# Scaling x and w_in so that the halves of g need no factor, and a list scheduler that knows more of its transfers

## The chip, the cores and the metric

The kernel runs on one core of a Trainium2 chip (trn2). The metric is the device time of one execution in microseconds. TensorE (PE) multiplies matrices, VectorE (DVE), ScalarE (ACT) and GpSimd (POOL) do elementwise work, SyncE (SP) issues nearly all transfers. Each engine runs its own queue of instructions in order and waits for others by semaphores.

## What is computed

```python
def _attn_ref(q, k, v):                      # (8, 8, 576, 64) each
    k_p = k.reshape(B, H, Sp, pool, D).mean(axis=3)      # pool = 8, Sp = 72
    v_p = v.reshape(B, H, Sp, pool, D).mean(axis=3)
    attn = softmax(np.matmul(q, k_p.transpose(0, 1, 3, 2)) / np.sqrt(D))
    return np.matmul(attn, v_p)
def _moe_ref(x, w_in, w_out, alpha):         # 4608 tokens, 512 -> 2048 -> 512
    h = x @ w_in
    g = np.maximum(h, 0.0) + alpha * np.minimum(h, 0.0)
    return g @ w_out
def _moe2_ref(x, w_gate, w1, w2):            # 8 experts, 512 -> 1024 -> 512, top 1
    logits = x @ w_gate
    ...
        h = np.maximum(xe @ w1[e], 0.0)
        out[mask] = gate_w[mask, None] * (h @ w2[e])
```

The three stages follow each other: the attention's output is x of the first, dense feed-forward block ("first MoE"), and that one's output goes to one of eight experts for each token ("second MoE").

## The kernel before

**Numbers.** Every matrix product is made of three float16 products: an operand a is split into a high half hi = f16(a s) and a low half lo = f16(a s - hi), and hi hi + hi lo + lo hi is summed in PSUM. `s_hi` (L183 on ACT, L185 on DVE, L187 on POOL) and `s_lo` (L198 on DVE; L200 and L201, two instructions, on POOL) make the halves. The scale s comes from a maximum over the operand: `inv_of` gives inv = max * 2^-14 and s = 1/inv; `over_all` takes a maximum over all partitions through a small matmul (tile `mp`, L308) and DVE (`dg` L304, `mr` L311).

**Stages.** Up to about 150 us w_in and w_out, which come as float64, are loaded, turned into float32 (L709 to L725; `w_in_t`, `w_out_t`), their maxima taken (L178, `absmax`) and split into `w_in_hl` and `w_out_hl`. w_in has four groups of columns with a scale each (`sw`), w_out one scale. The first MoE goes by 18 blocks of 256 tokens. `plan_tile` makes the attention of 128 tokens: q is loaded (`qr`, L528), scaled and split (`qs`), transposed by a transfer (`qT`), multiplied (`sc`), exponentiated on ACT (L574), normalised and split into `Abuf`, transposed (`AT`, L605) and multiplied with v (`xp`); its output is split into `xT`. `plan_in` makes 16 blocks `hp` of h (L804); for each two of them ACT makes relu(-h) (`r`, L818), DVE makes the activation in place (L822), then comes the high half of g (`gT`, by `s_hi` with the group's factor `cg`) and the low half (by `s_lo`). `r` has two buffers, `hp` three. `plan_out` multiplies with w_out (`yp`, L846) in four quarters. `plan_gate` splits the output (`x`), transposes it (`x2T`, L879), computes the gate (`gp`, L910), ranks the tokens (`rp`) and writes a table. `plan_expert` meanwhile splits the experts' weights (`ew` to `eo`) and stores them (`wsc`). From 1004 us on `plan_slots` takes 128 tokens at a time: it reads the table (`srec`, L1244), gathers (`x2g`, L1251), transposes (`x2gT`, L1264), multiplies with `ws` (L1276 and L1294) and scatters.

**Order.** Nothing of this is written in its final order. Each `plan_*` function adds operations to a plan, with the engines that may do them, an estimated duration, what they wait for, a key and the pools they take from and give back. `Plan.emit` is a list scheduler: it keeps a clock for each engine, takes the operation that can start first (ties by key), picks the engine, and so writes each engine's queue. SP's transfers have a rule of their own there, given by

```python
            if o.eng == "SP":
                dma = max(dma, t + 1.1) + o.dur
                e["t"] = max(t + 0.5, dma - AHEAD)
                o.end = dma + 0.95
```

so every transfer holds SP for 0.5 us and lands 0.95 us after its share of the DMA engines' time. The estimates set only the order; on the chip each instruction starts when its data are there.

Of the kernel before, what the change touches and what calls it, by code (L numbers as in the profile page):

```python
# [13 lines left out]
ACTF = mybir.ActivationFunctionType  # L14
# [18 lines left out]
class Op:  # L33
    __slots__ = ("eng", "dur", "fn", "deps", "key", "lat", "acq", "rel", "n", "users", "est", "end")
# [5 lines left out]
class Plan:  # L40
# [6 lines left out]
    def add(self, eng, dur, fn, deps=(), key=0.0, lat=0.0, acq=(), rel=(), order=()):  # L47
        o = Op()
        o.eng, o.dur, o.fn, o.key, o.lat, o.acq, o.rel = eng, dur, fn, key, lat, acq, rel
# [10 lines left out]
    def emit(self):  # L60
# [13 lines left out]
        while left:  # L74
# [57 lines left out]
def attn_moe_moe_kernel(ctx: ExitStack, tc: tile.TileContext, q, k, v, w_in, w_out, alpha,  # L132
# [263 lines left out]
    def alpha_c():  # L396
        mr = sm_["mr"]
        V.tensor_copy(cw[:, 0:1], mr[:, 0:1])
# [15 lines left out]
    def plan_batch(b, dl, users):  # L414
# [5 lines left out]
        for w in range(2):  # L420
            for c in range(nc_):
# [18 lines left out]
                o = add("SP", dmat(72 * 2048 * hn), load, key=dl - 28 + (8 * w + c) * 8 / nc_, acq=[(pl, 1)])  # L440
# [54 lines left out]
        oKT[b] = add("SP", 1.2, kT, [o2, o3, o4], key=dl - 4 - SPQ, acq=[("KT", 1)], rel=[("kc", 1)])  # L495
# [3 lines left out]
        o3 = add("SP", 0.5, vdma, [o1], key=dl - 4)  # L499
# [19 lines left out]
    def plan_tile(i):  # L519
# [99 lines left out]
        def xhi():  # L619
            if half == 0:  # L620
                xTt[j] = wk.tile([128, 2, KD, TB], F16, tag="xT", name="xT", bufs=2)
            s_hi(xTt[j][:, 0, :, sl], c["xp"], S14)

        def xlo():
            s_lo(xTt[j][:, 1, :, sl], xTt[j][:, 0, :, sl], c["xp"], S14)

        ends = [b for b in bs if LAST[b] == i]
        o = add("SP", dmat(262144) * 1.85, load, key=first(dl - 30, -6), acq=[("q", 1), ("att", 1)])
# [6 lines left out]
        o = add("SP", 1.0, q4, [o], key=dl - 16 - SPQ, acq=[("qT", 1)], rel=[("qs2", 1)])  # L635
# [13 lines left out]
        o = add("SP", 1.8, aT, [o1, o2], key=dl - 7 - SPA, acq=[("AT", 1)], rel=[("A", 1)])  # L649
# [8 lines left out]
    def plan_w(src, name, col, dl0, dl1, after):  # L658
# [83 lines left out]
        for g in range(ng):  # L742
# [8 lines left out]
            def scale(mg=mg, ig=ig, sg=sg):  # L751
                inv_of(mg, ig, sg)
# [15 lines left out]
        oW[name + "_s"] = add("DVE", tiny(4), scales3, o_s + [o_alpha, oW.get("w_in_s")], key=dl0 + 1)

        p1 = None  # L770
        for c in range(8):
            d = {}
            g = c * ng // 8

            def hi(eng, c=c, d=d, g=g):
# [18 lines left out]
    def plan_in(j):  # L794
        for m in range(KF):
# [651 lines left out]
```

## Time and profile before

| | |
|---|---|
| time, median of 3 runs | 1445.33 us (1442.6 to 1445.35) |
| the profiled execution | 1447.14 us, span 1445.4 us |
| PE busy | 1266.9 us (88%) |
| DVE, ACT, POOL busy | 891.2, 592.7, 778.7 us (62, 41, 54%) |
| mean granted TensorE clock | 0.972 of full speed |

Shares of busy time are means over stages with different limits. An idle time is put down to the instruction whose semaphore came last, the releaser. A line of a helper, as L178 or L198, stands for many operations; the tile tells which one is meant. Half the clock's full speed is the lower of TensorE's two levels.

### The profile page before, as it was taken

The numbers are of one execution on the slowest core, as the hardware profiler recorded it, in microseconds if no ns is written. First come the engines' busy times: TensorE is split into PE (matmuls) and PEld (weight loads), VectorE is DVE, ScalarE is ACT, GpSimd is POOL, SyncE is SP. The second block draws the span as 40 slices with busy tenths as digits, with TensorE's granted clock in tenths as the row PEclk, the third lists the DMA queues.
The fourth block names the chain that finished last, engine by engine and source line by source line (L and its number), as shares of the span: only waits on it lengthen the run. The fifth ranks groups of instructions, "written<-read, shape, count | busy, mean of one in ns | idle before, by whom it ended". The sixth has DMA issues, their size and how long they took to land. (4 is left out here: it accounts for less than half of the span.)

```text
span 1445.4 us, 30543 instructions
## 1 busy us (share of the span) xinstructions
PE 1266.9 (88%) x11555; PEld 875.0 (61%) x11555; DVE 891.2 (62%) x2051; ACT 592.7 (41%) x1324; POOL 778.7 (54%) x847
## 2 busy tenths in 40 slices
PE   0157799889898989999899999999799999999997
PEld 0145455646655755666576667765676776777674
DVE  7998788779667968868877777654252332332222
ACT  3786555536454645645564556541010110110010
POOL 6788967668677867647665666464122122112111
PEclk9998999999999999999999999999999999999999
DMA  9983397766777766676577476536658843593334
GB/s 241 290 196 91 98 222 149 191 152 163 190 149 171 201 190 130 176 195 153 126 189 199 122 149 146 172 103 197 168 133 240 198 91 74 167 304 104 74 96 166
DMA packets 314504, 237.21 MB, mean 164 GB/s; under 512 B 258351, under 2 KB 267695, under 8 KB 309488
## 3 DMA queue, kind: packets, MB, share of 16 engines
q1 hardware_dynamic: 306800, 214.98, 59.7%
q0 software_dynamic: 7552, 20.23, 4.7%
q8 instruction: 92, 1.51, 0.5%
q14 instruction: 60, 0.49, 0.1%
HBM read 263.52 MB, written 54.34 MB: 220 GB/s over the span
## 5 line engine op out<-in xcount | busy, mean ns | idle before, releaser
L804 PE MATMUL hp<-xT,w_in_hl 128*128 128x256 f16 x3456 | 409.8, 280 | 30.0 <-DVE r L822 22.4
L846 PE MATMUL yp<-w_out_hl,gT 128*128 128x512 f16 x1728 | 394.7, 386 | 9.6 <-POOL w_out_hl L201 5.4
L804 PEld LDWEIGHTS <-w_in_hl 128*128 128x128 f16 x3456 | 341.5, 100 | 83.1 <-DVE r L822 31.0
L846 PEld LDWEIGHTS <-gT 128*128 128x128 f16 x1728 | 168.2, 99 | 211.6 <-issue 22.6
L1276 PE MATMUL hp<-x2gT,ws 128*128 128x128 f16 x3744 | 217.9, 222 | 12.7 <-DMA x2gT<-x2g 8.1
L1276 PEld LDWEIGHTS <-ws 128*128 128x128 f16 x3744 | 215.7, 99 | 17.9 <-issue 12.0
L1294 PE MATMUL op<-ws,ht 128*128 128x512 f16 x936 | 205.7, 379 | 1.9 <-issue 1.9
L1282 ACT ACTIVATE hr<-hp 128x512 f32<-128x512 f32 x78 | 46.6, 597 | 374.1 <-PE hp L1276 369.9
L1294 PEld LDWEIGHTS <-ht 128*128 128x128 f16 x936 | 90.7, 98 | 107.6 <-issue 2.4
L574 ACT ACTIVATE e<-sc,nb,esc 128x72 f32<-128x72 f32 x288 | 116.3, 417 | 92.8 <-DVE inv L276 55.0
L1251 POOL DMA_INDIRECT x2g<-x2d,srec x41 | 43.5, 1061 | 202.3 <-DMA srec<-table 147.2
L822 DVE SCALAR_TENSOR_TENSOR r<-r,al,hp 128x256 f32<-128x256 f32 x288 | 124.0, 471 | 29.4 <-ACT r L818 29.1
L437 POOL TENSOR_TENSOR raw<-raw 72x256 f32<-72x256 f32 (+3 forms) x144 | 98.8, 686 | 65.2 <-DMA raw<-in_v_dram 30.4
L201 POOL TENSOR_TENSOR gT<-r,gT 128x512 f16<-128x512 f32 x99 | 124.8, 1260 | 8.3
L1286 DVE CAST ht<-hr 128x512 f16<-128x512 f32 x78 | 33.5, 430 | 151.5 <-ACT hr L1282 150.0
L183 ACT ACTIVATE gT<-r,cg 128x512 f16<-128x512 f32 x144 | 103.6, 724 | 55.9 <-DVE r L822 32.1
L183 ACT ACTIVATE eo<-ew,es 128x512 f16<-128x512 f32 x128 | 85.9, 713 | 97.7 <-DMA wsc<-eo 49.9
L1304 POOL DMA_INDIRECT out_dram<-so,srec x39 | 39.3, 1008 | 157.4 <-DVE cb L1299 60.4
L1301 DVE TENSOR_SCALAR so<-op,cb 128x512 f32<-128x512 f32 x39 | 29.3, 751 | 145.4 <-PE op L1294 145.3
L818 ACT ACTIVATE r<-hp 128x512 f32<-128x512 f32 x144 | 86.1, 598 | 75.0 <-POOL gT L201 49.4
L200 POOL TENSOR_SCALAR r<-r,cg 128x512 f32<-128x512 f32 x99 | 76.5, 772 | 60.9 <-ACT gT L183 59.9
L201 POOL TENSOR_TENSOR eo<-ew,eo 128x512 f16<-128x512 f32 x61 | 85.0, 1394 | 5.1
(221 smaller groups left out, 1524.9 us busy)
## 6 DMA issues: line engine op xcount, KB each, us to landing
ws<-wsc SPq DMA_DIRECT2D x166, 1024.0 KB
ew<-in_moe_w_dram SPq DMA_DIRECT2D x32, 1024.0 KB
wsc<-eo SPq DMA_DIRECT2D x64, 512.0 KB
x2d<-x SPq DMA_DIRECT2D x36, 256.0 KB
qr<-in_q_dram SPq DMA_DIRECT2D x32, 256.0 KB
w_in_f<-in_moe_w_in_dram SPq DMA_DIRECT2D x16, 512.0 KB
w_out_f<-in_moe_w_out_dram SPq DMA_DIRECT2D x16, 512.0 KB
raw<-in_k_dram SPq DMA_DIRECT2D x56, 144.0 KB
```

The lines of the kernel that those rows point to most:

```text
L183: A.activation(out=hi, in_=src, func=ACTF.Copy, scale=s)
L200: G.tensor_scalar(out=src, in0=src, scalar1=s, scalar2=0.0, op0=ALU.mult, op1=ALU.add)
L201: G.tensor_tensor(out=lo, in0=src, in1=hi, op=ALU.subtract)
L437: G.tensor_tensor(out=r[:, :, 0:n], in0=r[:, :, 0:n], in1=r[:, :, n:2 * n], op=ALU.add)
L574: A.activation(out=c["e"][x], in_=c["scv"][x], func=ACTF.Exp, bias=c["nb"][:, z // 4, z % 4:z % 4 + 1], scale=c["esc"], accum_out=c["sm"][x])
L804: T.matmul(out=hp, lhsT=wt[:, a, kk, (m % 4) * 128:(m % 4 + 1) * 128], rhs=xTt[j][:, x, kk, :], start=(n == 0), stop=(n == 3 * KD - 1))
L818: A.activation(out=c["r"], in_=hps[j, m // 2], func=ACTF.Relu, scale=-1.0)
L822: V.scalar_tensor_tensor(out=c["r"][:, z], in0=c["r"][:, z], scalar=al1[:, m - 1 + z:m + z], in1=hps[j, m // 2][:, z], op0=ALU.mult, op1=A ...
L846: T.matmul(out=ypt[i], lhsT=gT[j][x][:, m, o_ * 128:(o_ + 1) * 128], rhs=W["w_out"][part][:, w, m % 4, :], start=(m == 0 and x == 0 and w ...
L1276: T.matmul(out=hp[:, f, :], lhsT=ws[kk // 2][:, kk % 2, a, ff * 128:(ff + 1) * 128], rhs=c["xT"][:, x * KD + kk, :], start=(z == 0), stop= ...
L1282: A.activation(out=c["hr", f4], in_=c["hp", f4], func=ACTF.Relu, scale=S24)
L1294: T.matmul(out=op, lhsT=c["ht"][:, x, f, :], rhs=ws[f // 4][:, f % 4, w, :], start=(f == 0 and x == 0 and w == 0), stop=(f == KF2 - 1 and ...
```

## The change

x and w_in are scaled so that their halves' product is h times a known constant for each group of columns. The constant of `xT` becomes 2^-26 instead of 2^-14, and the scale of each group of w_in takes in alpha's bound (a quarter of it, `cw`). With that g's high half is a plain copy of `r` to float16 and its low half a plain difference; no factor is read, and POOL needs one instruction instead of two. The groups' factors `cg` are multiplied into w_out's scale instead, so w_out's halves wait for `scales3` of w_out. The scale of each group of w_in now waits for alpha.

The second part is in the planner. `ISSUE` is how long a transfer of a kind holds SP (0.45 us for the rest), `LATE` what its landing takes beyond the rule above; the gather's and the table's latency go from 2.5 to 3.3 and 4.0 us. No key is changed.

```diff
+ISSUE = {"qT": 1.4, "AT": 1.9, "yT": 1.4, "kT": 1.5, "xT": 1.4, "v": 1.6, "tok": 0.8}
+LATE = {"kv": 1.5, "q": 1.0, "ew": 2.5, "st": 1.0, "qT": 1.0, "AT": 1.2, "yT": 1.0, "kT": 0.8, "v": 2.0, "x2": 2.0, "xT": 1.0}
...
-                e["t"] = max(t + 0.5, dma - AHEAD)
-                o.end = dma + 0.95
+                e["t"] = max(t + ISSUE.get(o.kind, 0.45), dma - AHEAD)
+                o.end = dma + 0.95 + LATE.get(o.kind, 0.0)
...
-            s_hi(xTt[j][:, 0, :, sl], c["xp"], S14)
+            s_hi(xTt[j][:, 0, :, sl], c["xp"], S26)
...
-                inv_of(mg, ig, sg)
+                inv_of(mg, ig, sg, cw[:, 0:1] if is_in else S14)
...
-            o_s.append(add("DVE", tiny(2), scale, [o], key=key))
+            o_s.append(add("DVE", tiny(2), scale, [o, o_alpha], key=key))
...
                 V.tensor_tensor(out=cw[:, 4:5], in0=cw[:, 5:6], in1=iw, op=ALU.mult)
+                V.tensor_scalar(out=cg, in0=cg, scalar1=sw[:, 0:1], scalar2=None, op0=ALU.mult)
...
-            o = p1 = add(ANY, his(1024), hi, [o_s[g], p1], key=first(key - 1, 122), acq=[("big", 1)] if c % 2 == 0 else [])
+            o = p1 = add(ANY, his(1024), hi, [o_sc, p1], key=first(key - 1, 122), acq=[("big", 1)] if c % 2 == 0 else [])
...
-                s_hi(gT[j][0][:, n2], c["r"], cg[:, m * NGRP // KF:m * NGRP // KF + 1], eng)
+                if eng == "ACT":
+                    A.activation(out=gT[j][0][:, n2], in_=c["r"], func=ACTF.Copy)
+                else:
+                    on(eng).tensor_copy(gT[j][0][:, n2], c["r"])
...
-                s_lo(gT[j][1][:, n2], gT[j][0][:, n2], c["r"], cg[:, m * NGRP // KF:m * NGRP // KF + 1], eng)
+                on(eng).tensor_tensor(out=gT[j][1][:, n2], in0=c["r"], in1=gT[j][0][:, n2], op=ALU.subtract)
...
-            o = oGh[j] = add(ANY, his(512), ghi, [o, oW["w_in_s"], oGh.get(j)], key=key + 2, acq=[("big", 2)] if m == 1 else [])
-            oG[j, m // 2] = add(EITHER, stt(512), glo, [o], key=first(key + 2, -22), rel=[("r", 1)])
+            o = oGh[j] = add(ANY, (act(512),) + his(512)[1:], ghi, [o, oGh.get(j)], key=key + 2, acq=[("big", 2)] if m == 1 else [])
+            oG[j, m // 2] = add(EITHER, (dve(512), pool(512)), glo, [o], key=first(key + 2, -22), rel=[("r", 1)])
```

The new durations make the scheduler write every engine's queue anew. Three places follow, each engine's rows before and then now.

POOL in the steady stage, before: each low half of g is a row on `r` and a row on `gT`.

```order
L200 TENSOR_SCALAR r<-r,cg 128x512
L201 TENSOR_TENSOR gT<-r,gT 128x512
L586 TENSOR_TENSOR e<-e,sm 128x576
L200 TENSOR_SCALAR r<-r,cg 128x512
L201 TENSOR_TENSOR gT<-r,gT 128x512
L437 TENSOR_TENSOR raw<-raw 72x256
L437 TENSOR_TENSOR raw<-raw 72x128
L439 TENSOR_TENSOR kp<-raw 72x64
```

Now, at a like place:

```order
L842 TENSOR_TENSOR gT<-r,gT 128x512 x2
L592 TENSOR_TENSOR e<-e,sm 128x576
L205 TENSOR_SCALAR kp<-kp,s 72x512
L206 TENSOR_TENSOR vlo<-kp,VSb 72x512
L601 TENSOR_TENSOR Abuf_97<-e,Abuf_97 128x8x72
L842 TENSOR_TENSOR gT<-r,gT 128x512
L443 TENSOR_TENSOR raw<-raw 72x256
L443 TENSOR_TENSOR raw<-raw 72x128
```

The rows on `r` are gone; products of the softmax (`e`), k's and v's halves and sums (`raw`, `kp`) and the experts' halves (`ew`, `eo`) fill POOL as before.

DVE at the start, before: from the softmax of tile 2 (`sm`, `nb`) over w_in's last chunk (`w_in_t`, its maximum in `m_98`) to `xT` of the first block's second 128 tokens, which is the row L198.

```order
L198 SCALAR_TENSOR_TENSOR w_in_hl<-w_in_t,sw_100,w_in_hl 128x4x256
L579 TENSOR_SCALAR sm<-sm 128x8
L562 TENSOR_REDUCE mx<-sc 128x8
L582 RECIPROCAL sm<-sm 128x8
L566 TENSOR_SCALAR nb<-mx,esc 128x8
L721 SCALAR_TENSOR_TENSOR w_in_t<-wc,w_in_t 128x1024
L725 SCALAR_TENSOR_TENSOR w_in_t<-w_in_f_397,w_in_t 128x1024
L178 TENSOR_REDUCE m_98<-w_in_t 128x1
L198 SCALAR_TENSOR_TENSOR xT<-xp,xT 128x4x128
```

Now, the last rows up to the same `xT` (L203); w_in's last chunk and its maximum stand ahead of these rows, with the first of the two chunks of w_out:

```order
L309 TENSOR_SCALAR dg<-idb,iw_99 128x128
L727 SCALAR_TENSOR_TENSOR w_out_t<-wc,w_out_t 128x1024
L585 TENSOR_SCALAR sm<-sm 128x8
L568 TENSOR_REDUCE mx<-sc 128x8
L316 TENSOR_REDUCE mr_101<-mp 128x1
L588 RECIPROCAL sm<-sm 128x8
L572 TENSOR_SCALAR nb<-mx,esc 128x8
L731 SCALAR_TENSOR_TENSOR w_out_t<-w_out_f_494,w_out_t 128x1024
L179 TENSOR_SCALAR iw_99<-mr_101,cw 128x1
L180 RECIPROCAL sw_100<-iw_99 128x1
L183 TENSOR_REDUCE m_102<-w_out_t 128x1
L203 SCALAR_TENSOR_TENSOR xT<-xp,xT 128x4x128
```

Two chunks of w_out, their maxima (`m_102`) and the scale of w_in's last group stand between w_in's last maximum and `xT` now, and one low half of w_in (`w_in_hl`) no longer stands in front.

SP at the hand-over from the first MoE to the second, before, from behind the first gathered tile's transpose to the second's (ISA and TENSOR_LOAD rows read registers):

```order
L1230 TENSOR_LOAD regsA
L1230 ISA x2
L1238 ISA
L1238 DMA ws_1_12748<-wsc 128x4096
L1238 ISA
L1238 DMA ws_1_12749<-wsc 128x4096
L879 DMA_TRANSPOSE x2T<-x_12766 128x8x128
L1242 TENSOR_LOAD regsA
L1242 ISA x2
L1244 ISA
L1244 DMA srec<-table 128x2
L1264 DMA_TRANSPOSE x2gT<-x2g 128x8x128
```

Now, from a read of the table to the first weight load behind the two transposes:

```order
L1254 ISA
L1254 DMA srec<-table 128x2
L889 DMA_TRANSPOSE x2T<-x_12635 128x8x128
L1274 DMA_TRANSPOSE x2gT<-x2g 128x8x128 x2
L1240 TENSOR_LOAD regsA
L1240 ISA x2
L1248 ISA
L1248 DMA ws_1_12696<-wsc 128x4096
L1248 ISA
L1248 DMA ws_1_12697<-wsc 128x4096
```

The two transposes of gathered tiles stand together now, behind the transpose of one tile of `x` instead of around it, and ahead of the weight loads.

On TensorE the maximum over w_in's last group (`mp`) moves from behind three blocks of the first in-projection to in front of the second 128 tokens' attention product; the maximum over w_out moves from behind 11 of the second block's 16 in-projections to behind 6; a gate's matmul moves back by one in-projection in most blocks; an attention product moves back at first and from about the tenth block on forward by a quarter of an out-projection; and the count over the experts moves back by two in-projections.

## Rows read from the trace of the kernel before

**Rows 1.** Busy time of each engine in four stretches, with granted clock.
```profile
core 0: us, PE busy (x) PEld busy (x) DVE busy (x) ACT busy (x) POOL busy (x), PEclk, DMA share, GB/s
0.00:84.00 84.00, 8.71 (x104) 6.78 (x105) 71.11 (x119) 52.13 (x101) 61.07 (x73) 1.00 0.99 251
84.00:205.00 121.00, 95.33 (x708) 62.10 (x708) 98.46 (x183) 72.53 (x124) 100.87 (x100) 0.93 0.53 141
205.00:1004.00 799.00, 744.99 (x6043) 499.78 (x6041) 590.93 (x1461) 420.71 (x1022) 534.97 (x597) 0.97 0.67 164
1004.00:1042.00 38.00, 28.43 (x310) 22.41 (x311) 9.75 (x30) 3.78 (x7) 4.08 (x5) 0.87 0.75 195
```

**Rows 2.** Whom TensorE waited for from 84 to 205: us, times, longest.
```profile
PE hp L804 <- DVE r L822: 7.1, 4, 2.2
PE xp L614 <- DMA AT<-Abuf: 6.7, 1, 6.7
PE yp L846 <- POOL w_out_hl L201: 5.4, 3, 4.1
```

**Rows 3.** The same from 205 to 1042 us.
```profile
PE xp L614 <- DMA AT<-Abuf: 16.5, 9, 3.2
PE hp L804 <- DVE r L822: 15.3, 9, 5.3
PE gp L910 <- DMA x2T<-x: 10.1, 4, 3.2
PE hp L1276 <- DMA x2gT<-x2g: 5.9, 1, 5.9
```

**Rows 4.** Whom ScalarE waited for, 205 to 1005 us.
```profile
ACT e L574 <- DVE inv L276: 50.7, 11, 8.6
ACT r L818 <- POOL gT L201: 36.8, 28, 6.1
```

**Rows 5.** Whom VectorE waited for, 205 to 1005 us.
```profile
DVE m L178 <- DMA qr<-in_q_dram: 41.1, 11, 6.9
```

**Rows 6.** Timeline from 372 us: start, us; idle before and its releaser in brackets.
```profile
372.22 0.69 DVE L178 TENSOR_REDUCE m<-qr 128x1 f32<-128x512 f32 x1 [4.58 <-DMA qr<-in_q_dram]
376.91 7.08 PE L804 MATMUL hp<-xT,w_in_hl 128*128 128x256 f16 x48 [3.80 <-DVE r L822]
```

**Rows 7.** Groups by line and shape: count, busy us, mean ns; idle before.
```profile
L200 POOL TENSOR_SCALAR r<-r,cg 128x512 f32<-128x512 f32 x99 | 76.5, 772 | 60.9 <-ACT gT L183 59.9 <-ACT lg L942 0.4
L201 POOL TENSOR_TENSOR gT<-r,gT 128x512 f16<-128x512 f32 x99 | 124.8, 1260 | 8.3
L183 ACT ACTIVATE gT<-r,cg 128x512 f16<-128x512 f32 x144 | 103.6, 724 | 55.9 <-DVE r L822 32.1 <-DVE mt L932 5.4 <-DVE inv L174 4.0
L198 DVE SCALAR_TENSOR_TENSOR gT<-r,cg,gT 128x512 f16<-128x512 f32 x45 | 46.5, 1034 | 1.4 <-ACT gT L183 1.2
L1287 DVE TENSOR_TENSOR ht<-hr,ht 128x512 f16<-128x512 f32 x78 | 54.1, 694 | 2.7
L595 DVE TENSOR_TENSOR Abuf<-e,Abuf 128x576 f16<-128x576 f32 x11 | 11.3, 1028 | 0.0
L721 DVE SCALAR_TENSOR_TENSOR w_out_t<-wc,w_out_t 128x1024 int32<-128x1024 int32 x8 | 13.3, 1666 | 0.6 <-ACT w_out_t L713 0.6
```

**Rows 8.** Timeline of VectorE and TensorE at the start.
```profile
75.15 2.63 DVE L198 SCALAR_TENSOR_TENSOR w_in_hl<-w_in_t,sw,w_in_hl 128x1024 f16<-128x1024 f32 x1
82.03 1.22 DVE L178 TENSOR_REDUCE m<-w_in_t 128x1 f32<-128x1024 f32 x1
83.17 0.68 DVE L198 SCALAR_TENSOR_TENSOR xT<-xp,xT 128x512 f16<-128x512 f32 x1
83.90 5.82 PE L804 MATMUL hp<-xT,w_in_hl 128*128 128x256 f16 x35 [1.69 <-DVE xT L198]
```

**Rows 9.** Timeline of SyncE's queue at the hand-over.
```profile
1005.05 7.39 SPq L879 DMA_TRANSPOSE x2T<-x  x1
1013.70 2.94 SPq L1264 DMA_TRANSPOSE x2gT<-x2g  x1
```

More of the change, by code (lines that the diff above doesn't have):

```diff
@@ L33 @@
 class Op:
-    __slots__ = ("eng", "dur", "fn", "deps", "key", "lat", "acq", "rel", "n", "users", "est", "end")
+    __slots__ = ("eng", "dur", "fn", "deps", "key", "lat", "acq", "rel", "n", "users", "est", "end", "kind")
     def alts(self):
@@ L45, in __init__, with add @@
         self.ops, self.pools = [], pools
-    def add(self, eng, dur, fn, deps=(), key=0.0, lat=0.0, acq=(), rel=(), order=()):
+    def add(self, eng, dur, fn, deps=(), key=0.0, lat=0.0, acq=(), rel=(), order=(), kind=None):
         o = Op()
+        o.kind = kind
         o.eng, o.dur, o.fn, o.key, o.lat, o.acq, o.rel = eng, dur, fn, key, lat, acq, rel
@@ L397, in alpha_c @@
         mr = sm_["mr"]
-        V.tensor_copy(cw[:, 0:1], mr[:, 0:1])
+        V.tensor_scalar(out=cw[:, 0:1], in0=mr[:, 0:1], scalar1=0.25, scalar2=None, op0=ALU.mult)
         V.tensor_scalar(out=al1, in0=al1, scalar1=-1.0, scalar2=1.0, op0=ALU.mult, op1=ALU.add)
@@ L439, in reduce @@
                     G.tensor_tensor(out=o_, in0=r[:, :, 0:D], in1=r[:, :, D:2 * D], op=ALU.add)
-                o = add("SP", dmat(72 * 2048 * hn), load, key=dl - 28 + (8 * w + c) * 8 / nc_, acq=[(pl, 1)])
+                o = add("SP", dmat(72 * 2048 * hn), load, kind="kv", key=dl - 28 + (8 * w + c) * 8 / nc_, acq=[(pl, 1)])
                 red.append(add(EITHER, (0.15 + hn * 0.87, pool(448 * hn) + 0.6), reduce, [o] + red[-1:],
@@ L621, in xhi @@
                 xTt[j] = wk.tile([128, 2, KD, TB], F16, tag="xT", name="xT", bufs=2)
-            s_hi(xTt[j][:, 0, :, sl], c["xp"], S14)
+            s_hi(xTt[j][:, 0, :, sl], c["xp"], S26)
         def xlo():
-            s_lo(xTt[j][:, 1, :, sl], xTt[j][:, 0, :, sl], c["xp"], S14)
+            s_lo(xTt[j][:, 1, :, sl], xTt[j][:, 0, :, sl], c["xp"], S26)
         ends = [b for b in bs if LAST[b] == i]
-        o = add("SP", dmat(262144) * 1.85, load, key=first(dl - 30, -6), acq=[("q", 1), ("att", 1)])
+        o = add("SP", dmat(262144) * 1.85, load, kind="q", key=first(dl - 30, -6), acq=[("q", 1), ("att", 1)])
         o = add("DVE", dve(512), q1, [o], key=dl - 18)
@@ L888, in plan_gate @@
             o = add("DVE", dve(512), y3, [o], key=k_, rel=[("y", 1)])
-            o = add("SP", 1.0, y4, [o], key=k_ - SPY, acq=[("x2T", 1)])
+            o = add("SP", 1.0, y4, [o], kind="yT", key=k_ - SPY, acq=[("x2T", 1)])
             oT.append(o)
-            oS.append(add("SP", dmat(262144), y5, [o], key=k_ + 1, rel=[("x2", 1)]))
+            oS.append(add("SP", dmat(262144), y5, [o], kind="x2", key=k_ + 1, rel=[("x2", 1)]))
         def ct_(t, p0, n, b):
@@ L1056, in store @@
             Y.dma_start(out=wsc[r:r + 128, 2048 * c:2048 * (c + 1)], in_=cv[c].rearrange("p n c f -> p (n c f)"))
-        lds = [add("SP", dmat(1 << 20), lambda c=c: load(c), [oW["w_out"][-1]], key=t0 + c, acq=[("ew", 1), ("big", 1)]) for c in range(2)]
+        lds = [add("SP", dmat(1 << 20), lambda c=c: load(c), [oW["w_out"][-1]], kind="ew", key=t0 + c, acq=[("ew", 1), ("big", 1)]) for c in range(2)]
         for x in lds:
@@ L1327, in plan_slots @@
                 tt = "big"
-            o = add("SP", 0.1, tok, [o_r] + o_tab, key=key - 20, acq=[("srec", 1)])
-            o = oGa[n] = add("POOL", 1.1, gather, [o] + o_x2, key=key - 18, lat=2.5, acq=[(tg, 1)])
-            o_x = add("SP", 1.0, xT, [o], key=key - 15, acq=[(tt, 3 if tt == "big" else 1)], rel=[(tg, 1)])
+            o = add("SP", 0.1, tok, [o_r] + o_tab, kind="tok", key=key - 20, acq=[("srec", 1)])
+            o = oGa[n] = add("POOL", 1.1, gather, [o] + o_x2, key=key - 18, lat=3.3, acq=[(tg, 1)])
+            o_x = add("SP", 1.0, xT, [o], kind="xT", key=key - 15, acq=[(tt, 3 if tt == "big" else 1)], rel=[(tg, 1)])
             oXt[n] = o_x
```

30 lines of the change are left out of this document (16 added, 14 removed).

## The prediction

> **What bounds the kernel now.** I read the windows first, then who TensorE waits for, then the other engines' waits, then the groups by line. From 84 us on TensorE is the bound: between 205 and 1004 us it is busy 745.0 of 799 us, while DVE has 590.9, ACT 420.7 and POOL 535.0 [rows 1]. So time can come from two places there: its idle time, and the granted clock, which falls to the lower of its two levels (1.2 instead of 2.4 GHz) behind some stalls. The idle time is 121 - 95.3 = 25.7 us from 84 to 205, 54.0 us from 205 to 1004 and 9.6 us from 1004 to 1042. The clock's mean of 0.93, 0.97 and 0.87 in the same stretches is 0.07 x 121 + 0.03 x 799 + 0.13 x 38 = 8.5 + 24.0 + 4.9 = 37.4 us of missing clock [rows 1]. Before 84 us TensorE has 8.7 us of work, and DVE is busy 71.1 of 84 us [rows 1]: there the chains of DVE, ACT and transfers set the time. The second MoE behind 1042 us runs gapless and is not touched in its arithmetic.
>
> What TensorE waits for [rows 2, 3]: for the first MoE's activation (hp behind DVE's `r`) 7.1 + 15.3 us, for the transposed attention AT 6.7 + 16.5, for x2T 10.1, for w_out's halves 5.4, for a gathered tile x2gT 5.9.
>
> The waits for `r` have a history. ACT waits 36.8 us, 28 times, before L818, because the two buffers of `r` are still held by POOL's low half of g; and it waits 50.7 us before the exponentials, for DVE's scale of q [rows 4]. That scale is late because DVE, in order, stands before `m<-qr` until q's load lands: 41.1 us in 11 waits [rows 5]. At 372 us the reader sees it whole: DVE waits 4.58 us for q, ACT stands behind DVE with its relu queued behind the exponentials, and TensorE stops 3.80 us at 376.91 [rows 6]. The planner had that load landed earlier than it was, and put too little other work in front of the instruction that needs it.
>
> **The change, part by part.**
>
> *g's halves without a scale.* On POOL each low half is two instructions now, 772 and 1260 ns [rows 7]; the first goes. 99 x 0.772 = 76.5 us of POOL, and, what counts, about 0.77 us less for which each buffer of `r` is held. The order shows the planner giving part of POOL's room to others: 13 more expert low halves and 8 more products of the softmax stand on POOL, and as many fewer on DVE, so that DVE is relieved too. On DVE the low half becomes a TENSOR_TENSOR instead of a SCALAR_TENSOR_TENSOR of 1034 ns [rows 7]. Its price lies between 694 ns (L1287, same shape, in the second MoE) and 1028 x 512/576 = 914 ns (L595, in the same stage); I take 914, since there as here POOL is at work beside it: 43 x 0.12 = 5 us, with 15 as the other end. The Trainium skill (VectorE: DVE Perf Modes, The TRN2 errata) gives an fp32 tensor_tensor of 512 columns about 691 ns; by that alone the gain would be 15 us. The trace shows that figure only where POOL is nearly idle [rows 7]. On ACT the high half drops the scale read from memory: 724 ns now [rows 7], and L183's other groups bound it at no gain and at 0.13 us each, 0 to 19 us of 420 busy. None of this is on the chain by itself; it pays where TensorE waits for `r`. Of those 22.4 us I take 13: the holding of `r` (the 36.8 us on ACT) goes for the larger part, the waits behind q for a smaller.
>
> *The planner's transfers.* q's load is planned to land 1.0 us later, the transposes hold SP for 1.4 to 1.9 us instead of 0.5 and land 1.0 to 1.2 us later. 41.1 us in 11 waits for q are 3.7 us each [rows 5], so 1.0 us cures a quarter of each. Of x2T's 10.1 us in 4 waits I take 5: the gate's matmul moves back by about one block of in-projection in the order. AT's 23.2 us are 10 waits; its place in the order moves back early on, and forward by one quarter of an out-projection later on, so I take a third, 8 us; the bounds are 0 and 23.
>
> *w_out's rows take the factors.* Its halves wait for two more small DVE instructions, but in TensorE's order the maximum over w_out stands behind 6 instead of 11 blocks of in1, so the halves are made earlier: 5 of 5.4 us [rows 2].
>
> *The start.* This part costs. DVE's order now has tile 0's xT, then w_in's chunk 7, then two chunks of w_out, and only then tile 1's xT, on which the first in-projection waits. Before, chunk 7's maximum ends at 82.03 + 1.22 = 83.25 and xT at 83.85 [rows 8]. One low half of w_in (2.63 us [rows 8]) no longer stands in front. Between the maximum and xT stand three instructions of L721's kind (1.67 us [rows 7]) and two maxima (1.22): 7.4 us. So xT starts at 83.25 - 2.63 + 7.4 = 88.0 instead of 83.17: 5 us late. TensorE's sum for the maximum of w_in's last group, now in front of tile 1's attention product, costs nothing beside that: of the instructions just named only a part stand ahead of it on DVE, so it is ready before xT. If xT came earlier, it would itself be the late one. What w_out does here it needn't do later, which the w_out term has. The new wait of each group's scale on alpha costs nothing: alpha's few instructions are among DVE's first, with w_in's chunks still to come in front of the first scale.
>
> *The hand-over.* On SP the gathered tile 1's transpose moves from behind two weight loads and an x2T transpose that held the queue 7.39 us [rows 9] to directly behind tile 0's. The wait of 5.9 us [rows 3] should go; an x2T now stands in front of tile 0's transpose instead, but its data are made while TensorE still has the last out-projection to do; were they late, both gathered tiles would queue behind it on SP, and TensorE would stand before the second MoE. The count over the experts, from which the gathers get their rows, also stands two blocks later in TensorE's order. So the bounds are 0 and 6 us, and I take 6, as the hold of 7.39 us is longer than the wait.
>
> **The sum.** 13 + 5 + 8 + 5 + 6 = 37 us of 89.3 idle. The clock's 37.4 us go with the stalls in proportion: 37 x 37.4/89.3 = 15.5. Together 52.5 us. But the order is another everywhere, and the keys were left as they were: new waits will stand at places that don't wait now. The planner that made the present order from its own durations still left 54 us in the steady stage, so I let half come back, 26 us; that is a choice, with nothing and all as its ends. Then 52.5 - 26 - 5 (the start) = 21 us. The profiled execution took 1447.14 us for a span of 1445.4, 1.8 us above the median of 1445.33; 1447.1 - 21 = 1426, or from the median 1424.
>
> **The rivals.** About 0.2% (2.9 us) is what a measurement here can tell from no change.
> - *Nearly all waits go*, since SP's true time per transpose puts q, AT and x2T right together. For it: the three hang on one queue. Against it: 1.0 us for q is a quarter of its waits. 52.5 less a tenth, less 5: about 1403. Chance 0.2.
> - *The planner's figures don't do what they say*: transfers land by what is ahead of them in the DMA queues, not by a constant, so the waits for q, AT and x2T only move (one x2T held SP for 7.39 us [rows 9]), and the gain of the halves pays for the start. 13 + 5 = 18 of idle, 7 of clock, half back, less 5: 7 us, 1438. If the halves give nothing either, 1445. Chance 0.15, a third of it within 0.2%.
> - *Slower: the start takes over.* DVE's queue at the start is the mechanism, and xT of tile 1 its place. If chunk 7 comes no earlier, and the three instructions in between run as long as the 2.63 us that the low half of w_in took there [rows 8], xT starts at 83.25 + 3 x 2.63 + 2 x 1.22 = 93.6, 10.4 us late; tiles 2 and 3, behind w_out's next chunks in the same queue, can lose as much again. For it: DVE has no idle time to speak of there (71.1 of 84 us) [rows 1]. Against it: a part is only moved from later. It decides from the point where the start costs more than the rest gives, 26 us by the sum, 13 if only half of that comes. With 20 us lost and 13 gained: 1452. Chance 0.13.
> - *The forecast*, 1410 to 1438: 0.52.
>
> **How the numbers follow.** The forecast is the likeliest case, 1424. Faster by over 0.2% (below 1442.4): 0.52 + 0.2 + 0.1 = 0.82; within: 0.05; slower: 0.13. The range leaves out the slower case and the lower end of the one in which nearly all waits go, 0.18 together: 1398 to 1447.
>
> **What would show it.** Right: no TENSOR_SCALAR on `r` in POOL; ACT's wait for POOL's gT below 15 us; hp's waits for `r` below 10; x2T's below 6; the first long run of hp matmuls at about 88 to 89 us instead of 83.90 [rows 8]; the x2gT wait near 1019 gone; the clock of 205 to 1004 at 0.98 or more. Wrong: the idle of that stretch still near 54 us under other names, or DVE's wait for q as long as now with `r` behind it, or a start that comes 10 us late and is not caught up by 205 us.

## The result, and the profile after

The changed kernel takes 1390.49 us (median of 4 runs, 1386.93 to 1391.88), the kernel before 1443.96 (1437.24 to 1445.35) beside it: a ratio of 0.9635, interval 0.9599 to 0.9671. It is 53 us faster, where 21 were forecast, and below the range. The profiled span is 1390.1 us (1445.4 before).

Where did they go? TensorE's first slot of the second MoE is at 955.87 us, 50.0 us earlier than the 1005.83 of before. The span is cut there and at 84 us. Each line gives the stretch, its length and the busy time of each engine, in the columns of [rows 1]. Before:

```profile
84.00:1005.83 921.83, 840.32 (x6750) 561.91 (x6750) 690.99 (x1649) 493.93 (x1146) 636.94 (x697) 0.97 0.65 161
1005.83:1445.40 439.57, 417.87 (x4702) 306.32 (x4702) 129.10 (x284) 46.68 (x79) 80.67 (x78) 0.98 0.58 153
```

and after:

```profile
84.00:955.87 871.87, 824.09 (x6767) 556.22 (x6767) 690.09 (x1638) 468.90 (x1137) 579.87 (x633) 0.98 0.71 170
955.87:1390.10 434.23, 417.47 (x4702) 306.00 (x4701) 128.73 (x284) 46.68 (x79) 83.21 (x78) 0.98 0.56 154
```

TensorE's idle time up to the second MoE fell from 921.83 - 840.32 = 81.5 to 871.87 - 824.09 = 47.8 us, that is by 33.7; its busy time, for the same matmuls, fell by 16.2, by the clock (0.97 to 0.98 of full speed). In the second MoE 21.7 us of idle time became 16.8. Together 33.7 + 16.2 + 4.9 = 54.8, and 0.4 of busy time: the 55.3 us between the spans. By the stages of [rows 1], after:

```profile
0.00:84.00 84.00, 7.15 (x87) 5.83 (x88) 70.99 (x118) 53.54 (x93) 68.76 (x78) 1.00 1.03 268
84.00:205.00 121.00, 108.23 (x853) 73.66 (x853) 107.66 (x216) 75.35 (x154) 96.21 (x101) 0.96 0.62 155
205.00:1004.00 799.00, 758.69 (x6393) 516.39 (x6391) 602.18 (x1494) 398.44 (x993) 492.21 (x541) 0.98 0.71 171
```

TensorE's waits from 84 to 205 us, which answer to [rows 2]:

```profile
PE sc L561 <- DMA KTb<-kc: 3.7, 1, 3.7
PE hp L811 <- DVE r L829: 3.3, 1, 3.3
```

and from 205 to 1042 us, for [rows 3]:

```profile
PE xp L620 <- DMA AT<-Abuf: 10.1, 7, 4.4
PE hp L1286 <- DMA x2gT<-x2g: 7.5, 2, 4.5
PE rp L973 <- DVE oh L945: 6.7, 6, 1.8
PE mp L313 <- DVE xT L203: 6.1, 4, 3.6
PE gp L920 <- DMA x2T<-x: 3.7, 2, 2.1
PE mp L313 <- DVE dg L309: 3.2, 5, 0.9
PE hp L1286 <- DMA ws<-wsc: 2.4, 1, 2.4
PE hp L811 <- DVE r L829: 0.6, 2, 0.4
```

The waits for `r` went from 22.4 to 3.9 us, AT's from 23.2 to 10.1, x2T's from 10.1 to 3.7, those for the halves of w_out that [rows 2] shows from 5.4 to none. These four fell by 43.4 us together. TensorE's idle time fell by only 33.7, so 9.7 us stand under other names now (`oh`, `mp`, `dg`, KTb), which are many and short.

What ScalarE waits for from 205 to 1005 us ([rows 4]): for POOL's low halves 12.9 instead of 36.8 us, and before the exponentials, under the name `inv`, 14.0 + 7.5 = 21.5 instead of 50.7 + 14.2 = 64.9 us. The 14.2 is a second line of before, with the other instruction that writes `inv`:

```profile
ACT e L574 <- DVE inv L272: 14.2, 2, 10.7
```

After:

```profile
ACT e L580 <- DVE inv L281: 14.0, 4, 6.3
ACT r L825 <- POOL gT L842: 12.9, 10, 2.8
ACT e L580 <- DVE inv L277: 7.5, 2, 6.0
```

VectorE's own wait for q, which the prediction had behind ScalarE's, is only a quarter shorter: 30.1 instead of 41.1 us [rows 5].

```profile
DVE m L183 <- DMA qr<-in_q_dram: 30.1, 11, 6.8
```

### The profile page after: what moved, and what is told of

Read it like the earlier page. It is cut to its first block, busy times and chain, and to the rows that moved or that the text cites. A ratio compares the mean times of both kernels' runs of the same rounds, so it can differ in the third digit from the quotient of the medians.

```text
span 1390.1 us, 30446 instructions
## 1 busy us (share of the span) xinstructions
PE 1248.7 (90%) x11555; PEld 868.0 (62%) x11555; DVE 889.8 (64%) x2039; ACT 569.1 (41%) x1309; POOL 731.8 (53%) x788
## 5 line engine op out<-in xcount | busy, mean ns | idle before, releaser
L811 PE MATMUL hp<-xT,w_in_hl 128*128 128x256 f16 x3456 | 395.9, 275 | 6.2 <-DVE r L829 3.9
L856 PE MATMUL yp<-w_out_hl,gT 128*128 128x512 f16 x1728 | 388.8, 383 | 1.2 <-DVE x L203 1.2
L811 PEld LDWEIGHTS <-w_in_hl 128*128 128x128 f16 x3456 | 336.6, 99 | 53.3 <-issue 6.8
L842 POOL TENSOR_TENSOR gT<-r,gT 128x512 f16<-128x512 f32 x101 | 121.5, 1207 | 74.1 <-ACT gT L837 70.9
L443 POOL TENSOR_TENSOR raw<-raw 72x256 f32<-72x256 f32 (+3 forms) x150 | 115.7, 772 | 38.8 <-DMA raw<-in_v_dram 17.2
L188 ACT ACTIVATE eo<-ew,es 128x512 f16<-128x512 f32 x125 | 83.6, 715 | 117.4 <-DMA wsc<-eo 44.2
L837 ACT ACTIVATE gT<-r 128x512 f16<-128x512 f32 x142 | 89.6, 633 | 65.3 <-DVE r L829 31.7
L205 POOL TENSOR_SCALAR ew<-ew,es 128x512 f32<-128x512 f32 x71 | 53.0, 746 | 60.4 <-ACT eo L188 59.9
```

The costliest lines, as they stand in the source:

```text
L188: A.activation(out=hi, in_=src, func=ACTF.Copy, scale=s)
L443: G.tensor_tensor(out=r[:, :, 0:n], in0=r[:, :, 0:n], in1=r[:, :, n:2 * n], op=ALU.add)
L811: T.matmul(out=hp, lhsT=wt[:, a, kk, (m % 4) * 128:(m % 4 + 1) * 128], rhs=xTt[j][:, x, kk, :], start=(n == 0), stop=(n == 3 * KD - 1))
L837: A.activation(out=gT[j][0][:, n2], in_=c["r"], func=ACTF.Copy)
L842: on(eng).tensor_tensor(out=gT[j][1][:, n2], in0=c["r"], in1=gT[j][0][:, n2], op=ALU.subtract)
L856: T.matmul(out=ypt[i], lhsT=gT[j][x][:, m, o_ * 128:(o_ + 1) * 128], rhs=W["w_out"][part][:, w, m % 4, :], start=(m == 0 and x == 0 and w ...
```

## The start and the hand-over

VectorE's timeline at the start, for [rows 8], has the two chunks of w_out in front of tile 1's `xT`:

```profile
77.82 1.22 DVE L183 TENSOR_REDUCE m<-w_in_t 128x1 f32<-128x1024 f32 x1
...
86.92 1.20 DVE L183 TENSOR_REDUCE m<-w_out_t 128x1 f32<-128x1024 f32 x1
88.04 0.68 DVE L203 SCALAR_TENSOR_TENSOR xT<-xp,xT 128x512 f16<-128x512 f32 x1
```

and TensorE begins its long run of in-projections when it has it:

```profile
88.77 6.50 PE L811 MATMUL hp<-xT,w_in_hl 128*128 128x256 f16 x36 [1.25 <-DVE xT L203]
```

That is 88.77 instead of 83.90. By the first gate the loss is more than made up: the gate's first matmul is at 185.43 us instead of 199.43. At the hand-over TensorE still stops three times, 9.8 us together:

```profile
955.87 8.15 PE L1286 MATMUL hp<-x2gT,ws 128*128 128x128 f16 x102 [4.51 <-DMA x2gT<-x2g]
966.37 3.62 PE L1286 MATMUL hp<-x2gT,ws 128*128 128x128 f16 x42 [2.35 <-DMA ws<-wsc]
...
981.73 4.20 PE L1286 MATMUL hp<-x2gT,ws 128*128 128x128 f16 x48 [2.94 <-DMA x2gT<-x2g]
```

On SP the pair of transposes now goes as one run, and the next x2T holds the queue for 3.82 us:

```profile
952.55 2.64 SPq L1274 DMA_TRANSPOSE x2gT<-x2g  x2
956.31 2.24 SPq L1248 DMA_DIRECT2D ws<-wsc  x2
958.66 0.36 SPq L892 DMA_DIRECT2D x2d<-x  x1
959.82 0.34 SPq L1254 DMA_DIRECT2D srec<-table  x1
960.27 3.82 SPq L889 DMA_TRANSPOSE x2T<-x  x1
```

## The experiments

They ran on four other chips, on each of which the kernel before takes 1428 to 1430 us; so each kernel's ratio to the kernel before on its own chip is compared. The expectations that are in us were made from the 1444 us of the first result, and are read here as shares of it. "Waits for loads" is added up from the views of the waits from 205 to 920 us: POOL's for k and v, VectorE's for k, v, q and the experts' weights. The last column is TensorE's busy time in that window; a higher clock shortens it, so it isn't the work done. The row of the kernel before is from its trace on the first chip.

| kernel | ratio, 95% interval | waits for loads, us | PE busy of 715 us |
|---|---|---|---|
| before | 1 | 111.8 | 662.0 |
| new halves, old order | 0.991 (0.988 to 0.994) | 110.6 | 673.1 |
| old halves, new order | 0.980 (0.976 to 0.983) | 48.7 | 679.6 |
| old halves, new planner | 0.966 (0.962 to 0.970) | 42.2 | 693.9 |
| new halves, old planner | 0.991 (0.988 to 0.994) | 84.1 | 674.8 |
| the change again | 0.967 (0.963 to 0.971) | 49.1 | 691.7 |
| issue times only | 0.990 (0.987 to 0.994) | 84.3 | 676.8 |
| landings only | 0.974 (0.970 to 0.977) | 44.0 | 688.0 |
| landings of loads only | 0.975 (0.970 to 0.981) | 35.4 | 675.8 |
| q's landing only | 0.990 (0.987 to 0.993) | 85.0 | 672.1 |
| experts' landing only | 0.988 (0.984 to 0.992) | 53.1 | 678.0 |
| k's and v's landing only | 0.984 (0.980 to 0.988) | 59.5 | 677.6 |
| the change, q at 3.0 | 0.972 (0.969 to 0.976) | 52.1 | 686.7 |
| a hopeful plan | 1.018 (1.015 to 1.021) | 141.4 | 653.2 |
| half the table | 0.985 (0.982 to 0.987) | 68.7 | 680.9 |
| 1.5 times the table | 0.968 (0.964 to 0.971) | 44.2 | 693.8 |
| twice the table | 0.972 (0.970 to 0.975) | 33.4 | 683.6 |

The two columns on the right are from one trace each. The changed kernel has two, and its first one, on the first chip, gives 58.7 us of waits for loads where the table has 49.1. Differences of 10 us in that column tell nothing. Nor does the column set the order of the ratios: 53.1 us go with 0.988, and those 58.7 with the first result's 0.964.

**Halves or order.** Theory A: the planner's new order brings the time. Theory B: the cheaper halves do. Two kernels cross the two parts. In them the scheduler's choice is replaced by a recorded list, and each operation is written where the list has it, or earlier where another needs it:

```diff
+        todo = [(v >> 3, ENGS[v & 7]) for v, in struct.iter_unpack("<H", raw)]
...
+        for i, _ in todo:
+            put(i)
```

The new halves in the order of before:

> The changed kernel's instructions, written in the queues' order of the kernel before (an operation is put earlier only where one that stands before it needs it). Theory A (the gain of 53 us is the new order, the shorter halves of g are worth what the prediction gave them, 13 us of waits for r and about 5 of clock): 1425 to 1432. Theory B (the halves alone free r and POOL, and the order would be worth little): 1395 to 1405. In both POOL has no TENSOR_SCALAR on r; A has the waits for AT, x2T and q as before.

The old halves in the new order:

> The kernel before, its instructions unchanged, written in the changed kernel's order of queues. Theory A: 1400 to 1412, since most stalls go with the order, and g's low half on POOL costs 0.77 us more each where the order had counted on less. Theory B: 1430 to 1450, as the order then fits an r that is held longer. If both parts need each other, it lies between, 1412 to 1430.

Then each part with a schedule of its own. The kernel before with the new table and latencies:

```diff
-                e["t"] = max(t + 0.5, dma - AHEAD)
-                o.end = dma + 0.95
+                e["t"] = max(t + ISSUE.get(o.kind, 0.45), dma - AHEAD)
+                o.end = dma + 0.95 + LATE.get(o.kind, 0.0)
...
```

> The kernel before with the table of the transfers' issue times and landings in the scheduler, and the two latencies, but g's halves as they were (with the durations the scheduler had for them). Theory A: 1400 to 1415. Theory B: 1430 to 1445.

The same diff turned round in the changed kernel:

> The changed kernel with the scheduler's old rule for transfers (0.5 us of SP, 0.95 us to land, latencies of 2.5 us): the scaling and the shorter halves alone, planned as such. Theory A: 1425 to 1435. Theory B: 1395 to 1405.

The halves are worth 0.9% at the old planning, in either order of the work: 0.991. The planner alone is worth 3.4%, all that the change is worth (0.966 against 0.967, the intervals overlap). So B falls, and A holds for the planner as a whole: 0.966 is even a little better than its range for that kernel (1400 to 1415 us, 0.970 to 0.980). The two parts don't add up. Once the plan is right, the cheaper halves bring nothing that can be measured. TensorE still waits for `r` there (205 to 920 us, old halves, new planner), but for little else:

```profile
PE hp L808 <- DVE r L826: 11.4, 6, 4.3
PE gp L914 <- DMA x2T<-x: 3.5, 4, 1.6
PE xp L618 <- DMA AT<-Abuf: 2.3, 1, 2.3
```

In return the changed kernel, run again, has 5.5 us for AT and 6.9 for `oh` in the same window. The old halves in the order made for the new ones get 0.980 and not 0.966. That is 1414 of 1444 us, at the edge between A's range and the one for parts that need each other. This order did better with the durations that it was made from; the old order did not, as the new halves get the same 0.991 in it as in one of their own.

**Issue or landing.** The landing is the moment at which a transfer's data have arrived. Theory C: SP's own time for a transpose, which keeps SP's queue true, carries the gain. Theory D: the landings do.

> The changed kernel itself, beside the parts of its table on the same chip: 0.960 to 0.967 of the kernel before, by every theory.

```diff
-LATE = {"kv": 1.5, "q": 1.0, "ew": 2.5, "st": 1.0, "qT": 1.0, "AT": 1.2, "yT": 1.0, "kT": 0.8, "v": 2.0, "x2": 2.0, "xT": 1.0}
+LATE = {}
...
```

> The changed kernel with the table of issue times alone (no later landings, latencies of 2.5 us). Theory C (what was wrong with the old plan is SP: a transpose holds it for 1.2 to 1.9 us and not 0.5, so everything behind it in SP's queue is late, q's loads with it): 0.965 to 0.972 of the kernel before, DVE's wait for q's loads between 205 and 940 us below 15 us. Theory D (it is the landings): 0.985 to 0.992, as with the halves alone, the wait for q still above 25 us.

Here the latencies of the gather and the table are the old 2.5 us as well. Landings with the new latencies, and no issue times:

```diff
-ISSUE = {"qT": 1.4, "AT": 1.9, "yT": 1.4, "kT": 1.5, "xT": 1.4, "v": 1.6, "tok": 0.8}
+ISSUE = {}
...
-                e["t"] = max(t + ISSUE.get(o.kind, 0.45), dma - AHEAD)
+                e["t"] = max(t + ISSUE.get(o.kind, 0.5), dma - AHEAD)
```

> The changed kernel with the later landings and latencies alone, every transfer holding SP for 0.5 us. Theory C: 0.980 to 0.990. Theory D: 0.962 to 0.972, DVE's wait for q's loads below 15 us.

Of the landings only those of loads, with issue times and latencies as before:

```diff
+ISSUE = {}
+LATE = {"kv": 1.5, "q": 1.0, "ew": 2.5}
...
```

> The changed kernel with later landings of the loads of k, v, q and the experts' weights alone (no later transposes, no issue times, latencies of 2.5 us). If the story of the prediction holds, that a load of q which lands later than planned stops DVE, ACT and at last TensorE, this has half or more of the landings' effect: below 0.980, and DVE's wait for q below 20 us, with the waits of TensorE for AT as in the kernel before, above 18 us. If the transposes are what counts: 0.985 to 0.993.

Issue times alone give nothing on top of the halves (0.990 against 0.991), so C falls. The landings give 1.7 of the 2.4% from 0.991 to 0.967, and those of three kinds of load nearly all of it (0.975), though TensorE's wait for AT is 19.8 us there, no shorter than the 16.5 of before. The rest needs both: the issue times help once the landings are there (1390 to 1394 us without, 1379 to 1386 with, on one chip).

**Which load.** Theory E: q, on which the prediction had looked. Theory F: the experts' weights, with the largest number. Each kernel has one entry of the last diff.

> The halves as changed, and of the whole table only q's landing, 1.0 us later. Theory E (a late load of q stops DVE, then ACT, then TensorE; one number in the plan takes that away): 0.975 to 0.982 of the kernel before, ACT's wait before the exponentials for DVE's scale (62 to 68 us where the loads are planned as before, 14 us with all loads later) below 30 us. Theory F (it is the experts' weights: 2 MB in front of the next transfers, and DVE's wait for them): 0.988 to 0.993, that wait above 50 us.

> The halves as changed, and only the experts' weights landing 2.5 us later. Theory E: 0.988 to 0.993, DVE's wait for the weights gone, ACT's wait for DVE's scale as before. Theory F: 0.975 to 0.983.

> The halves as changed, and only the loads of k and v landing 1.5 us later. Theories E and F: 0.988 to 0.993. Below 0.983 if it is the sums over k and v, which stand in DVE's and POOL's queues with everything else behind them.

And the change with q's entry at 3.0 instead of 1.0:

> The changed kernel with q's landing planned 3.0 us late instead of 1.0. Theory E: DVE's wait for q's loads, 22.9 us there, falls below 12, and the time to 0.955 to 0.965. If 1.0 us was enough to take q off the path, it stays at 0.967 (0.963 to 0.971).

E and F both fall. q's 1.0 us took VectorE's wait for q from 39.1 us (new halves, old planner) to 20.0 and moved the time by nothing (0.990). ScalarE's wait before the exponentials, expected below 30 us, was as long as ever:

```profile
ACT e L580 <- DVE inv L281: 74.3, 12, 11.5
```

The traces show a part of the reason. In the program the exponentials need `nb`, the scaled maximum of their scores, and not the `inv` that the view names: in each of the 13 waits before, they start 0.09 or 0.10 us after `nb`, and the `inv` of another chain happens to end beside it. `nb` needs the scores. Of the 65.0 us of these waits in the kernel before (205 to 920 us), 26.2 lie ahead of the moment at which TensorE had made the scores; in the rest VectorE stood idle for q's load for 8.3. With q's landing alone it is 52.5 of 77.7 us, and 3.0. In the changed kernel's first trace 13.1 of 21.5 lie ahead of the scores and none of VectorE's 30.1 us for q falls into the rest: that wait is still there, and ScalarE no longer stands behind it. A late q can make the scores late too, by its transpose; that isn't in these numbers. The place that the prediction looked at [rows 6] shows the same in small. ScalarE had stood for 10.66 us. q's load took 4.58 of them, between the maximum of the scores and `nb`, and a load of v had held VectorE for 2.02 in the same stretch:

```profile
365.28 1.04 DVE L433 TENSOR_REDUCE kp<-raw 72x64 f32<-72x512 f32 x1 [2.02 <-DMA raw<-in_v_dram]
373.20 0.41 ACT L574 ACTIVATE e<-sc,nb,esc 128x72 f32<-128x72 f32 x1 [10.66 <-DVE inv L272]
```

Three times as much for q in the changed kernel takes VectorE's wait for it nearly away, and the kernel is no faster for it, at 0.972 just above both ranges that were expected (VectorE's waits for loads of q and of experts' weights, 205 to 920 us):

```profile
DVE m L183 <- DMA qr<-in_q_dram: 3.9, 2, 2.4
DVE em L183 <- DMA ew<-in_moe_w_dram: 0.5, 1, 0.5
```

Of the three kinds k and v come out best, 0.984, just beside the range below 0.983 that was expected if they were the cause. Only their interval lies clear of the 0.991 (0.988 to 0.994) of the halves alone, and it overlaps that of the experts' weights, so the order of the two isn't shown. The three alone add up to 1.1% (0.7, 0.3 and 0.1), and together they give 1.6. The waits for k and v are ones that the prediction never named. Before, they were POOL's above all, as large together as q's 41.1 us [rows 5]:

```profile
POOL raw L437 <- DMA raw<-in_k_dram: 23.1, 11, 4.4
POOL raw L437 <- DMA raw<-in_v_dram: 20.1, 12, 3.1
```

POOL runs in order, and the low halves of g, which hold `r`, stand behind. In the changed kernel's first trace the same two lines are:

```profile
POOL raw L443 <- DMA raw<-in_v_dram: 10.1, 7, 2.4
POOL raw L443 <- DMA raw<-in_k_dram: 7.8, 4, 4.5
```

That this wait is the path of the gain isn't shown: with q's landing alone the two lines have 38.5 us, with the halves alone 25.7, at the same time.

**Truth or luck.** A scheduler that always takes what can start first gives another order for any new number. Theory G: the table was one lucky reshuffle. Theory D says that the closer the planned landing is to the true one, the better. Four doses of it, with the changed kernel's arithmetic in each; less than none first:

```diff
+ISSUE = {}
+LATE = {}
...
-                o.end = dma + 0.95 + LATE.get(o.kind, 0.0)
+                o.end = dma + 0.05
```

> The changed kernel's arithmetic with every transfer planned to land 0.05 us instead of 0.95 us after its share of the DMA engines' time, no table, the old latencies. Theory D (the planned landing drives the order: the later, up to the true one, the better): a more hopeful plan than the old rule's, so slower than the 0.991 that the old rule gives with these halves: 0.997 to 1.015, with VectorE's wait for q above 41 us and ScalarE's before the exponentials above 70. Theory G (luck: any change of a duration reshuffles a greedy order, and the measured table was one lucky shuffle): anywhere from 0.97 to 1.01, with no order among the four kernels of this set.

Half of what the table adds, one and a half times, and twice (the two latencies stay at the changed kernel's 3.3 and 4.0 us in these three):

```diff
+ISSUE = {'qT': 0.95, 'AT': 1.2, 'yT': 0.95, 'kT': 1.0, 'xT': 0.95, 'v': 1.05, 'tok': 0.65}
+LATE = {'kv': 0.75, 'q': 0.5, 'ew': 1.25, 'st': 0.5, 'qT': 0.5, 'AT': 0.6, 'yT': 0.5, 'kT': 0.4, 'v': 1.0, 'x2': 1.0, 'xT': 0.5}
```

> The changed kernel with half of the table's additions (issue times halfway to 0.5 us, landings at half). Theory D: between 0.991 (none) and 0.967 (all): 0.975 to 0.986, with VectorE's wait for q between 20 and 35 us. Theory G: outside that.

> The changed kernel with one and a half times the table's additions. Theory D: about that of the whole table, 0.963 to 0.972, with less wait for q (below 15 us) and a little given back elsewhere. Theory G: outside that.

> The changed kernel with twice the table's additions. Theory D: past the true landings nothing more is to be had, and room in the buffers is lost by loads that are issued earlier: 0.964 to 0.980, wait for q below 10 us. Theory G: outside that, and no order among the four.

From the most hopeful to the most careful plan the ratios are 1.018, 0.991, 0.985, 0.967, 0.968, 0.972: down to a flat foot at the table and half as much again, and slightly up behind it. The waits for loads fall along the row: 141.4, 84.1, 68.7, 49.1, 44.2, 33.4 us. The three steps down are each larger than the intervals. Behind them the curve is flat up to half as much again, and the last step up is small but real: the runs of the two kernels on one chip, 1378 to 1386 and 1388 to 1390 us, don't overlap. Without order G can't explain this, and it falls. What is shown is that planning the landings later helps up to about the table, and that later still costs little. That the best values are the true landings isn't shown by so flat a foot, and a plan with all transfers later by one amount was not tried. In detail D was off. VectorE's wait for q came out at 15.5 and 10.7 us with the larger tables, and at 19.5 with the landings only, where below 15, 10 and 15 had been expected. The hopeful plan lost even more than expected (1.018, at most 1.015 expected), and not at q (36.8 us, expected above 41) but at the experts' weights:

```profile
DVE em L183 <- DMA ew<-in_moe_w_dram: 37.1, 13, 7.0
DVE m L183 <- DMA qr<-in_q_dram: 36.8, 14, 5.6
```

Twice the table has the shortest waits for loads and isn't the fastest: ScalarE's wait before the exponentials is long again there, 44.5 us in 10 waits behind the same kind of instruction:

```profile
ACT e L580 <- DVE inv L281: 44.5, 10, 7.7
```

With a second line of 1.7 us ScalarE's waits come to 46.3 us there. Of these 29.4 lie ahead of the moment at which TensorE has made the scores, and in the rest VectorE doesn't stand idle for q. Why the scores come late there isn't shown.

A single load's landing can be read off where an engine stood waiting for it. Before, SP issued the q of [rows 6] here:

```profile
368.19 1.27 SPq L528 DMA_DIRECT2D qr<-in_q_dram  x1
```

and VectorE went on at 372.22: 4.03 us. That is also the median of the 11 such waits (3.25 to 7.17), if each is taken with the last load of its kind that SP issued before. The old rule plans 1.1 + 1.44 + 0.95 = 3.49 us for it with nothing ahead (1.44 is the planner's own figure for the bytes), the new one 4.49. For k and v it is 2.51 planned, 4.01 now, and about 3.6 as the median of POOL's 23 waits; for the experts' weights 5.01, 7.51, and 5.75 as the median of 7. These are the loads that were waited for, so the late ones, and what they spent behind other transfers is in them, which the plan counts apart. So the old rule was short by at most 0.5 to 1.1 us at these medians. The new one is on the careful side for them, though not for the longest. The Trainium skill (DMA: Bandwidth & Descriptors, Anatomy of one DMA) gives a transfer some 2.0 us beside its bytes at 436 GB/s, fitted there to transfers issued by GpSimd. An estimate from it is 2.6 us for q, 2.3 for k or v and 4.4 for the experts' weights; by that the old rule was long enough and the table would bring nothing. The runs disagree, for loads that SP issues among many others, and they decide.

No run points to a version that beats the changed kernel: the planner alone, the change and the table half as large again lie within each other's intervals, at 0.966 to 0.968.

## Why the prediction was off

The direction was right, and so was the cause in its main part, loads that were planned to land too early. The size was off by 32 us, through one step above all, and the paths by which the prediction had the gain come, q and the halves, were not the ones.

**The sum of the waits was near, and "I let half come back, 26 us" was wrong.** Its 37 us of idle time and 15.5 of clock, less 5 for the start, are 47.5. Up to the second MoE the trace has 33.7 less idle, with the start's loss in it, and 16.2 less busy by the clock: 49.9, and 4.9 more behind it. The four waits that the prediction cut there fell by 43.4 us, where it had taken 31. Under other names 9.7 us appeared, of which the start is 4.9. So 4.8 us came back in new places, not half. The reason given was that a new order makes new waits where none were. The runs show what it left out: this order was made from later landings, and a plan that has them too early pays in stalls (1.018 for the most hopeful one, 0.967 for the table, 0.966 for the table without the new halves). The rival "nearly all waits go", 1403 us with 0.2, was the nearest. Its sum gave a tenth of the 52.5 us back, and its condition, SP's true time per transpose, isn't what brings the gain: issue times alone have 0.990.

**The start**: tile 1's `xT` 5 us late at 88.0 us, measured 88.04, and the matmuls at 88.77 against 83.90. The place and the size are right, the hit to 0.1 us is in part luck. The maximum over w_in's last chunk ended at 79.04 us instead of the 80.62 of the sum, and 9.0 instead of 7.4 us lay between it and `xT`, as small instructions of the softmax stand there too. The lead at the first gate is 14 us.

**The waits for `r`**: 13 of 22.4 us taken, 18.5 gone. The cause was given wrongly for the larger part. The halves alone take `hp`'s waits from 205 to 920 us to 6.9 us but the time only to 0.991, and the planner alone leaves 11.4 and gets 0.966. Of the 13 "more expert low halves" on POOL that the prediction read from the order, ten came (61 to 71 in the traces).

**AT, x2T, w_out**: 8, 5 and 5 taken; 13.1, 6.4 and 5.4 gone.

**q**: "1.0 us cures a quarter of each" is what the first trace has (41.1 to 30.1 us), though in others the same 1.0 us takes more (39.1 to 20.0 alone). The step from there to TensorE failed. The exponentials don't wait for q's scale but for `nb`, VectorE's idle time for q held it back for only 8.3 of ScalarE's 65.0 us, and curing that wait alone gained nothing. What had to be counted were all loads that an engine runs in order behind; k, v and the experts' weights were not in the sum.

**The hand-over**: 6 us taken, 0.6 came (2.84, 5.91 and 1.70 us before, 9.8 together now). SP's hold went, and the gathered tiles were still late: 4.51 and 2.94 us in front of two of them.

**DVE's low half**: 914 ns taken with 694 as the other end, and the mean is 1039, no faster than the 1034 of the two-operation form [rows 7]. The means hide two kinds of instruction. The medians (in the middle of the three numbers) are 757 ns before and 693 after, so most are as fast as the other end, and a few long ones eat the gain. Before and after:

```profile
L198 DVE SCALAR_TENSOR_TENSOR gT<-r,cg,gT x45: 692/757/2024, 110.8 to 924.5; 128x512 f16<-128x512 f32 x45
L842 DVE TENSOR_TENSOR gT<-r,gT x43: 633/693/2917, 100.9 to 927.7; 128x512 f16<-128x512 f32 x43
```

The 914 came from such a mean too: L595's 1028 ns has a median of 746. And the prediction saw the 694 ns only where POOL is nearly idle; by the median they are there in the first MoE too.

**ACT's high half**, bounded by 0 and 0.13 us, gained 0.09:

```profile
L842 POOL TENSOR_TENSOR gT<-r,gT 128x512 f16<-128x512 f32 x101 | 121.5, 1207 | 74.1 <-ACT gT L837 70.9 <-DMA x2d<-x 1.6 <-DVE dg L309 0.6
L837 ACT ACTIVATE gT<-r 128x512 f16<-128x512 f32 x142 | 89.6, 633 | 65.3 <-DVE r L829 31.7 <-DVE pf L988 9.5 <-DVE oh L945 4.3
L842 DVE TENSOR_TENSOR gT<-r,gT 128x512 f16<-128x512 f32 x43 | 44.7, 1039 | 4.6 <-ACT gT L837 4.4
```

Of the signs named for right all came but one: the row on `r` is gone from POOL, ACT's wait for POOL (12.9), `hp`'s (3.9), x2T's (3.7), the start and the clock (0.98) are as said; the x2gT wait stayed.

## What to carry to other kernels

Where a list scheduler writes in-order queues, check when it believes that a load lands: measure issue to landing for each kind of load, put the measured value in rather than a hopeful constant, and lean to the late side. In this kernel twice the correction cost 0.5%, no correction 2.4%, and a plan 0.9 us more hopeful than that another 2.7%. Before you forecast such a change, list the waits for loads on every engine, also those off the critical path (POOL's 43 us for k and v here), and ask who stands behind each wait: q's cure, alone, was worth nothing, and most of q's wait was still there when the time had gone. Read the median beside the mean before you price an instruction. Two gains that feed the same wait don't add; here the cheaper halves (0.9%) vanished beside the better plan (3.4%).

## What was not expected of the hardware

The low half on VectorE, a plain fp32 difference of 512 columns, has a mean of 1039 ns, but 22 of the 43 took 0.63 to 0.69 us, as the like shape in the second MoE did (694 ns [rows 7]). The Trainium skill (VectorE: DVE Perf Modes, The TRN2 errata) gives about 691 ns for it; the median of 693 agrees. Each of the other 21 (0.73 to 2.92 us) overlaps an instruction on POOL, and several last about 0.54 us longer than what was left of it, as if they had waited for its end. Here POOL's ends at 205.40 and VectorE's at 205.94 us:

```profile
204.24 1.16 POOL L206 TENSOR_TENSOR qs<-qr,qs 128x512 f16<-128x512 f32 x1
204.67 1.27 DVE L842 TENSOR_TENSOR gT<-r,gT 128x512 f16<-128x512 f32 x1
```

Others beside a POOL instruction were not stretched; no run varied which of the two starts first. ScalarE's copy is 0.09 us shorter without a factor read from memory (633 instead of 724 ns).
